# Maxout over three products: one product moved behind the maximum, its share of the output through a matrix formed on chip, and a new order of the whole program

## The chip, the core and the metric

The kernel runs on one core of a Trainium2 chip. The metric is the time of one execution on the device, in microseconds (us). TensorE (PE) multiplies matrices into PSUM, VectorE (DVE) and ScalarE (ACT) work on PSUM and SBUF, GpSimd (POOL) works on SBUF and issues those transfers that change the type, SyncE (SP) issues transfers and transposing transfers.

## The reference

There are 8 batches (B), 8 heads (H), 512 rows of x and 32 rows of state per batch and head, 64 columns. All inputs and the output are float32; the kernel computes in bfloat16 and accumulates in float32.

```python
a  = softmax(x @ state.T / 8)           # per batch and head: 512 x 32
xread = a @ state                        # 512 x 64
a2 = softmax(state @ x.T / 8)           # 32 x 512
sread = a2 @ x                           # 32 x 64
t  = concat([xread, sread], rows)        # heads side by side: 8*544 rows of 512
h  = maximum(maximum(t @ w1, t @ w2), t @ w3)     # 768 columns
out = h @ w_out                          # 4352 rows of 512 columns
```

## The kernel before

The eight batches' xread rows (512 per batch) and the 256 state rows of all batches take two paths.

**Rows of x.** The kernel never forms xread. For a batch it multiplies the states with the weights, G = state @ [w1 w2 w3] for each head (`g_slice`, `g_run`, line 363: eight small matmuls of 64 x 32 tiles side by side), copies G from PSUM to bf16 (lines 381, 403, 406), and then layer 1 is G times the turned softmax weights aT. The 768 columns are six *slices* of 128. For a slice `layer1` makes three products of 512 columns, each of two matmuls (line 416), into three PSUM banks. `max_first` copies the first to SBUF on ACT (line 431); `max_second` takes the maximum with the second on DVE (line 436); `max_third` with the third (line 440), into `ht`. `layer2` (line 447) then makes an output tile of 128 rows as six matmuls over the slices, one PSUM bank; `layer2_out` copies it to SBUF (line 454), and stores take it out.

**Before that**, per batch: x is loaded with a cast by POOL (lines 163, 168), turned by a transposing DMA on SP (line 249; batches 0 and 1 on PE, line 237), multiplied with the states to scores (line 262), exponentiated on ACT (line 269); sums and reciprocals on DVE (276, 278); weights `a` on POOL (line 284), turned into aT by another transposing DMA (line 302). `sread` (line 327) makes the state rows, with a copy of x padded by ones on POOL (line 311); they are scaled, turned by DMA and placed in `atp`.

**State rows.** All 256 go together through layer 1 (`layer1_states`, four matmuls of 256 columns for each of three products and six slices) and layer 2 at the end.

**The order** of every engine's work is written out by hand as a text: FIRST for the start, EACH once per batch 2 to 6, LAST for the end. Each word is one of the functions in `table`. An engine executes its instructions in the order of that text, and waits where an operand or a buffer is not ready; so do the transfers of a queue behind each other. `busy n` is n filler matmuls on zeros (line 211). PSUM has four single banks and two pairs; BANKS and PAIRS name the one that each use takes. The weights come by POOL's queue in column slices (`lw`, line 179), `w_out` by one transfer behind them (`lwo`, line 184), x of batches 2 and up between them.

At the end a matmul with ones gathers a flag that decides about a second path for extreme inputs, which isn't taken here.

Of the kernel before, what the change touches and what calls it, by code (L numbers as in the profile page):

```python
# [17 lines left out]
FIRST = """  # L18
    lst 0 A; lxu 0 0 S; zero; clr 0; clr 1; clr 2; clr 3; warm; lxg 0 1; busy 1; xones 1; ident; busy 1;
    lxg 1 0; busy 1; busy 1; stc 0 D; busy 1; busy 1; busy 1; busy 1; busy 1; lxg 1 1; stt 0; busy 2;  # L20
    cxu 0 0 D; xt 0 0; stp 0 A; busy 1; xt 0 1; busy 1; xtc 0 0 D; lw 0 2 1; lw 0 2 2; xtc 0 1 D;
    busy 1; sc 0 0; busy 1; lw 0 1 0; busy 1; sc 0 1; lw 1 3 0; ex 0 0; busy 1; busy 1; xt 1 0; sum 0 0;
    lw 2 3 1; busy 1; ex 0 1; sum 0 1; xt 1 1; busy 1; xtc 1 0 AD; busy 1; lw 2 3 2; busy 1; xtc 1 1 A;
    busy 1; wt 0 0 P; wt 0 1 P; xones 0; sc 1 0; ex 1 0; busy 1; sc 1 1; at 0 0; atc 0 0 A; sr 0;
    busy 1; sum 1 0; lw 3 4 0; at 0 1; lst 1 A; lw 3 6 2; lw 3 6 1; ex 1 1; wt 1 0 D; g 0 0; gc 0 0 D;
    busy 1; sum 1 1; g 1 0; sr 1; atc 0 1 A; lw 4 6 0; wt 1 1 P; at 1 0; srs 0; g 1 1; g 0 1; stc 1 P;
    l1 0 0; gc 1 1 D; gc 1 0 A; g 1 2; g 0 2; atc 1 0 A; busy 1; gc 0 1 A; m0 0 0; at 1 1; lxg 2 1;
    srs 1; ma 0 0; l1 0 1; lxg 2 0; gc 0 2 A; l1 0 2; atc 1 1 D; l1 1 0; m0 0 1; m0 0 2; lwo; m0 1 0;
    gc 1 2 A; mb 0 0; xtd 2; l1 1 1; g 0 3; m0 1 1; lst 3 S; lst 2 A; ma 0 1; gc 0 3 A; g 1 3; pad 2;
    stt 1; gc 1 3 A; mb 0 1; ma 0 2; mb 0 2; ma 1 0; mb 1 0; l1 1 2; ma 1 1; g 0 5; m0 1 2; ones; g 0 4;  # L30
    mb 1 1; stp 1 DA; l1 0 3; gc 0 4 A; ma 1 2; g 1 4; gr 2 1792 2304; gc 0 5 D; m0 0 3; mb 1 2; l1 1 3;
    l1 0 5; gc 1 4 A; gr 2 0 512; g 1 5; m0 1 3; ma 0 3; mb 0 3; ma 1 3; l1 1 4; grc 2 1792 2304 A;
    mb 1 3; m0 0 5; gr 2 1280 1792; stc 2 P; lxg 3 1; gr 2 512 1024; ma 0 5; l1 0 4; stt 2; sc 2 -;
    gc 1 5 A; m0 1 4; grc 2 0 512 D; mb 0 5; lxg 3 0; ma 1 4; grc 2 1280 1792 AD; m0 0 4; ma 0 4;
    mb 0 4; mb 1 4; xtd 3; l2 0 3; l2 0 1; ex 2 -; l1 1 5; stp 2 A; l2c 0 3 D; stc 3 P; l2 0 2; sum 2 -;
    l2c 0 1 D; stt 3; l2 0 0; m0 1 5; ma 1 5; l2c 0 2 A; grc 2 512 1024 D; wt 2 - P; sr 2; mb 1 5;
    srs 2; gr 2 1024 1280; l2c 0 0 D; so 0 0 2 P; lx 4; so 0 2 4 P; stp 3 A; grc 2 1024 1280 A; atd 2;
"""
EACH = """
    pad 1; gr 1 1792 2304; gr 1 0 512; grc 1 1792 2304 AD; l2 -1 0; l2 -1 1; l1 0 0; grc 1 0 512 D;  # L40
    l2c -1 0 A; m0 0 0; sc 1 -; l2 -1 3; gr 1 1024 1280; ex 1 -; xtd 2; gr 1 1280 1792; l2c -1 1 D;
    ma 0 0; gr 1 512 1024; mb 0 0; sr 1; grc 1 1024 1280 A; l1 0 1; l1 0 2; sum 1 -; l1 0 3; srs 1;
    l1 0 5; l2c -1 3 A; m0 0 1; m0 0 2; ma 0 1; mb 0 1; ma 0 2; m0 0 3; mb 0 2; srt -2; ma 0 3;
    wt 1 - P; m0 0 5; mb 0 3; l2 -1 2; grc 1 1280 1792 A; grc 1 512 1024 A; ma 0 5; mb 0 5; l2c -1 2 D;
    l1 0 4; so -1 2 4 P; m0 0 4; ma 0 4; lx 3; mb 0 4; atd 1; ap -2 A; so -1 0 2 P;
"""
LAST = """
    srt 6; l1 7 0; srt 7; l2 6 0; l1 7 2; m0 7 0; l1 7 3; l1 7 4; ap 7 D; m0 7 2; srt 5; ap 6 A; ma 7 0;
    m0 7 3; mb 7 0; ap 5 A; l2c 6 0 D; ma 7 2; l2 6 1; l1s 0; l2 6 2; m0 7 4; mb 7 2; l1 7 1; l2c 6 1 A;
    ma 7 3; m0 s 0; l2c 6 2 A; l1s 2; l1 7 5; ma 7 4; mb 7 4; look; ma s 0; m0 7 1; m0 s 2; mb s 0;  # L50
    so 6 2 3 S; m0 7 5; mb 7 3; l1s 1; ma 7 1; mb 7 1; ma s 2; mb s 2; ma 7 5; m0 s 1; ma s 1; l1s 5;
    so 6 0 1 S; mb 7 5; l2p 7 2 384 512; l1s 3; m0 s 5; ma s 5; mb s 1; m0 s 3; mb s 5;
    l2pc 7 2 384 512 A; l2p 7 0 384 512; l2p 7 3 256 512; sop 7 2 384 512 P; ma s 3; l2p 7 2 128 384;
    mb s 3; l2p 7 0 0 128; l2pc 7 0 0 128 A; l2pc 7 3 256 512 D; l2p 7 1 0 128; l2p 7 3 0 256;
    l2pc 7 0 384 512 D; flag; l2pc 7 1 0 128 A; l2pc 7 2 128 384 A; l1s 4; m0 s 4; l2 6 3;
    sop 7 0 0 128 P; ma s 4; sop 7 0 384 512 P; mb s 4; l2p s 0 256 512; so 6 1 2 P; l2 s 1;
    sop 7 3 256 512 A; l2c 6 3 D; l2p 7 2 0 128; sop 7 1 0 128 S; l2p s 0 0 256; so 6 3 4 A;
    l2pc 7 3 0 256 D; l2pc s 0 256 512 D; sop s 0 256 512 A; l2pc 7 2 0 128 A; l2p 7 1 128 384;
    sop 7 2 0 128 A; l2p 7 0 256 384; l2p 7 1 384 512; l2pc s 0 0 256 A; l2p 7 0 128 256;
    l2pc 7 1 128 384 A; l2c s 1 D; sop 7 3 0 256 S; sop 7 2 128 384 P; l2pc 7 0 256 384 D;  # L60
    sop 7 1 128 384 A; l2pc 7 1 384 512 D; sop 7 1 384 512 A; l2pc 7 0 128 256 D; sop 7 0 128 256 A;
    sos 1 S; sop s 0 0 256 S; sop 7 0 256 384 S; hold; vl;
# [6 lines left out]
"""  # L69
PAIRS = """  # L70
    0101100101 1010010010 1010101010 1010101010 10
# [4 lines left out]
def kernel(  # L76
# [35 lines left out]
    times = {"D": nc.vector.tensor_mul, "P": nc.gpsimd.tensor_mul}  # L112
    queue = {"S": nc.sync, "P": nc.gpsimd, "A": nc.scalar}
# [9 lines left out]
    w_sb = data.tile([128, HS, 3, d_ff], BF16, name="w")  # L123
# [10 lines left out]
    xT, e, a, aT, G, ht, osb, xp = {}, {}, {}, {}, {}, {}, {}, {}  # L134
    open_ps = {}

    def new(d, b, shape, name, bufs=2):
        d[b] = work.tile(shape, BF16, tag=name, bufs=bufs, name=name)


    homes = {n: iter("".join(t.split())) for n, t in (("b", BANKS), ("w", PAIRS))}
# [28 lines left out]
    def load_x_uncast(b, g, q):  # L170
        o = work.tile([128, J, d_model], F32, tag="osb", bufs=3, name="osb")
        x_f[b, g] = o.rearrange("p j f -> p (j f)")[:, 0:HS * J * D].rearrange("p (s jd) -> p s jd", s=HS)
        queue[q].dma_start(out=x_f[b, g], in_=x_heads(b, g))
# [4 lines left out]
    def load_w(m0, m1, i):  # L178
        nc.gpsimd.dma_start(  # L179
            out=w_sb[:, :, i, m0 * 128:m1 * 128],  # L180
            in_=(moe_w1, moe_w2, moe_w3)[i].rearrange("(kk p) f -> p kk f", p=128)[:, :, m0 * 128:m1 * 128])

    def load_wout():
        nc.gpsimd.dma_start(out=wout_sb, in_=moe_w_out.rearrange("(kk p) f -> p kk f", p=128))
# [46 lines left out]
    def x_turn(b, g):  # L231
        if g == 0:
            new(xT, b, [128, H, 2, 128], "xT", bufs=3)
# [7 lines left out]
    def x_turned(b, g, c):  # L241
        p, w = open_ps.pop(("x", b, g)), HS // len(c)
# [4 lines left out]
    def x_turn_dma(b):  # L247
        new(xT, b, [128, H, 2, 128], "xT", bufs=3)
        nc.sync.dma_start_transpose(out=xT[b].rearrange("p h j t -> p (h j) t"), in_=x_sb[b][:, 0:XW])

# [3 lines left out]
    def scores(b, g=None):  # L254
        if not g:
            new(e, b, [128, J, 2, HS, Ns], "e")
# [11 lines left out]
    def exps(b, g=None):  # L268
        nc.scalar.activation(out=parity(e[b], g), in_=open_ps.pop(("s", b, g)), func=AF.Exp, scale=scale)  # L269
# [10 lines left out]
    def weights(b, g, c):  # L280
        if not g:
            new(a, b, [128, J, 2, HS, Ns], "a")
# [7 lines left out]
    def a_turn(b, g):  # L290
        if g == 0:
            new(aT, b, [128, J, 2, 128], "aT", bufs=3)
# [4 lines left out]
    def a_turned(b, g, c):  # L297
        copier[c](out=aT[b][:, :, g, :], in_=open_ps.pop(("a", b, g)))

    def a_turn_dma(b):  # L300
        new(aT, b, [128, J, 2, 128], "aT", bufs=3)
# [4 lines left out]
    def pad(b):  # L306
        xp[b] = work.tile([128, HS, J, 2 * D + 2], BF16, tag="xp", name="xp")
# [7 lines left out]
    def sread(b):  # L315
        w = D + 1 if b in xp else 2 * D
        p = open_ps["r", b] = bank([128, 2, w], F32, "psr")
        for j in range(J):
            for g in range(2):
                for s in range(HS):  # L320
                    if b in xp:
                        both = xp[b][:, s, j, g * D:g * D + D + 1]
                    else:
# [4 lines left out]
                        p[32 * s:32 * s + 32, g], e[b][:, j, g, s, :], both,  # L328
# [31 lines left out]
    def g_mm(b, p, f):  # L360
        for s in range(HS):
            for g in range(2):
                nc.tensor.matmul(  # L363
                    p(s, g), bd(b, 2 * s + g)[64 * g:64 * g + 64, g, :], f(w_sb[64 * g:64 * g + 64, s]),
                    start=True, stop=True, tile_position=(64 * g, 32 * s))

    def new_g(b):
        if b not in G:
            new(G, b, [128, 2, 3, d_ff], "G", bufs=3)


# [26 lines left out]
    def g_ran(b, c0, c1, c):  # L398
# [5 lines left out]
        else:  # L404
            for g in range(2):
                copier[c[g % len(c)]](out=v[:, g], in_=ps[g][:, 0:c1 - c0])
# [271 lines left out]
```

## Time and profile before

| | |
|---|---|
| time, median of 3 runs (lowest to highest) | 152.66 us (152.51 to 152.88) |
| span of the profiled execution, first to last instruction | 151.4 us |
| PE busy | 146.4 us (97%) |
| DVE busy | 118.9 us (79%) |
| ACT busy | 82.8 us (55%) |
| POOL busy | 57.0 us (38%) |
| moved by DMA | 22.29 MB |

Times in a view of the profile are microseconds from the span's start, unless marked as ns. The profiled execution is one of the program's; its own time isn't recorded beside its span, so that the median, 1.24 us above the span, stands for it. Matmuls are pipelined: the mean duration of one, 379 ns, is longer than the distance from one to the next, which the chain of waits shows. The lines themselves stand in the prediction.

### The profile page before, as it was taken

The page shows a single profiled execution, that of the slowest core. Times are in us where ns is not written, and L with a number is a line of the kernel's source. Part 1 is how long each engine was busy: PE and PEld are TensorE (multiplying, and loading weights), DVE is VectorE, ACT ScalarE, POOL GpSimd, SP SyncE. Part 2 cuts the span into 40 slices and gives each one's busy share as a digit, 9 for nine tenths or more (in the row PEclk, how much of TensorE's full clock was granted, in tenths as well). Part 3 has the DMA queues.
Part 4 walks back from the last instruction along what each step waited for, and adds up shares of the span by engine and source line. Part 5 has one row for each costly group of instructions (what it writes and reads, how often), then busy time and mean ns, then how long its engine had stood idle before and what let it go on. Part 6 is the DMA issues. An engine that isn't in the chain of part 4 may idle for free.

```text
span 151.4 us, 3635 instructions
## 1 busy us (share of the span) xinstructions
PE 146.4 (97%) x1431; PEld 73.8 (49%) x1431; DVE 118.9 (79%) x204; ACT 82.8 (55%) x143; POOL 57.0 (38%) x79
## 2 busy tenths in 40 slices
PE   6999799999999999999999999999999999999992
PEld 2566343335445443544354435443544446679771
DVE  6477698999977898879987988798879887675353
ACT  3368558976364665466646664666466653331220
POOL 6979650561528505540554046414331200001500
PEclk9999999999999999999999999999999999999999
DMA  3999999979737979999589749974503250300455
GB/s 115 211 189 195 207 198 195 151 149 139 139 74 167 230 59 265 129 223 132 155 124 230 144 130 140 232 122 141 218 0 78 68 226 4 122 18 17 175 180 196
DMA packets 39108, 22.29 MB, mean 147 GB/s; under 512 B 23072, under 2 KB 36896, under 8 KB 39088
## 3 DMA queue, kind: packets, MB, share of 16 engines
q0 software_dynamic: 15872, 13.96, 48.7%
q1 hardware_dynamic: 21776, 6.82, 23.4%
q10 hardware_dynamic: 1440, 1.25, 2.7%
q8 instruction: 12, 0.20, 0.5%
q14 instruction: 8, 0.07, 0.2%
HBM read 15.20 MB, written 8.91 MB: 159 GB/s over the span
## 4 chain that ended last, share of the span: by engine, by line
PE 86%; DMA 6%; POOL 4%; issue 1%; DVE 1%; POOLq 0%
PE pw L416 46%; PE po L447 25%; DMA w<-in_moe_w_dram 6%; PE pg L363 5%; PE po L462 4%; POOL w L179 2%; PE ps L262 2%; PE psr L327 2%; POOL x L168 1%; PE pgh L363 1%; PE pt L222 1%; DVE held L522 0%; PE idle L520 0%; PE idle L211 0%; DVE osb L466 0%
## 5 line engine op out<-in xcount | busy, mean ns | idle before, releaser
L416 PE MATMUL pw<-aT,G 128*128 128x512 bf16 x288 | 66.8, 379 | 0.0
L431 ACT CAST t<-pw 128x512 bf16<-128x512 f32 (+1 forms) x54 | 30.4, 564 | 28.9 <-PE pw L416 27.2
L416 PEld LDWEIGHTS <-G 128*128 128x128 bf16 x288 | 27.2, 98 | 33.2 <-issue 1.9
L436 DVE TENSOR_TENSOR t<-t,pw 128x512 bf16<-128x512 bf16 (+1 forms) x54 | 35.4, 655 | 9.5 <-ACT t L431 7.4
L447 PE MATMUL po<-wout,ht 128*128 128x512 bf16 x168 | 39.9, 379 | 0.0
L440 DVE TENSOR_TENSOR ht<-t,pw 128x512 bf16<-128x512 bf16 x48 | 32.9, 687 | 4.3
L447 PEld LDWEIGHTS <-ht 128*128 128x128 bf16 x168 | 15.3, 98 | 19.0 <-issue 1.7
L284 POOL TENSOR_TENSOR a<-e,rden 128x1024 bf16<-128x1024 bf16 (+1 forms) x9 | 14.5, 1620 | 24.1 <-ACT osb L454 11.1
L477 POOL DMA_DIRECT2D out_dram<-osb x13 | 7.4, 572 | 30.5 <-ACT t L431 27.5
L403 ACT CAST G<-pg 128x1024 bf16<-128x1024 f32 (+1 forms) x17 | 14.3, 875 | 1.3 <-PE pg L363 1.3
L311 POOL COPY xp<-x 128x1024 bf16<-128x1024 bf16 x12 | 12.3, 1062 | 5.5 <-DMA x<-in_x_dram 5.5
L454 DVE COPY osb<-po 128x512 f32<-128x512 f32 x16 | 10.9, 684 | 2.4 <-PE po L447 2.3
L276 DVE TENSOR_REDUCE seen<-e 128x32 f32<-128x1024 bf16 (+1 forms) x10 | 10.0, 999 | 3.6 <-ACT e L269 3.6
L403 DVE CAST G<-pg 128x1024 bf16<-128x1024 f32 (+1 forms) x13 | 12.2, 972 | 0.7 <-ACT G L403 0.7
L454 ACT COPY osb<-po 128x512 f32<-128x512 f32 x13 | 7.7, 593 | 8.9 <-PE po L447 8.9
L269 ACT ACTIVATE e<-ps 128x1024 bf16<-128x1024 f32 (+1 forms) x10 | 8.5, 854 | 6.6 <-PE ps L262 6.4
L363 PE MATMUL pg<-w,bd 64*32 64x512 bf16 (+1 forms) x288 | 10.8, 362 | 0.9 <-DMA w<-in_moe_w_dram 0.9
L211 PE MATMUL idle<-zero 128*128 128x512 bf16 x27 | 10.0, 477 | 1.3 <-DVE zero L187 1.3
L472 POOL DMA_DIRECT2D out_dram<-osb x4 | 2.2, 544 | 19.4 <-ACT osb L466 19.4
L381 ACT CAST G<-pg 128x768 bf16<-128x768 f32 x9 | 7.1, 801 | 3.3 <-PE pg L363 3.1
L416 PE MATMUL pw<-atp,w 128*128 128x256 bf16 x72 | 8.7, 272 | 0.0
L416 PEld LDWEIGHTS <-w 128*128 128x128 bf16 x72 | 6.9, 98 | 1.5
(70 smaller groups left out, 116.0 us busy)
## 6 DMA issues: line engine op xcount, KB each, us to landing
out_dram<-osb POOLq DMA_DIRECT2D x12, 512.0 KB, 3.5
x<-in_x_dram POOLq DMA_DIRECT2D x4, 512.0 KB, 7.3
x<-in_x_dram POOLq DMA_DIRECT2D x7, 256.0 KB, 5.5
w<-in_moe_w_dram POOLq DMA_DIRECT2D x4, 256.0 KB, 7.5
w<-in_moe_w_dram POOLq DMA_DIRECT2D x2, 384.0 KB, 7.9
wout<-in_moe_w_out_dram POOLq DMA_DIRECT2D x1, 768.0 KB, 11.6
out_dram<-osb SPq DMA_DIRECT2D x3, 256.0 KB, 2.4
osb<-in_x_dram SPq DMA_DIRECT2D x1, 512.0 KB, 4.0
```

Source lines behind the costliest of these rows:

```text
L211: nc.tensor.matmul(p, zero[:, 0:128], zero, start=True, stop=True)
L276: nc.vector.reduce_sum(out=den, in_=parity(e[b], g), axis=AX.X)
L284: times[c](out=parity(a[b], g).rearrange("p j g s n -> p j (g s) n"), in0=parity(e[b], g).rearrange("p j g s n -> p j (g s) n"), in1=rdens ...
L311: nc.gpsimd.tensor_copy(out=xp[b][:, :, :, g * (D + 1):g * (D + 1) + D], in_=v[:, g])
L363: nc.tensor.matmul(p(s, g), bd(b, 2 * s + g)[64 * g:64 * g + 64, g, :], f(w_sb[64 * g:64 * g + 64, s]), start=True, stop=True, tile_positi ...
L403: copier[c[g]](out=v[:, g:h], in_=p[:, g:h, 0:c1 - c0])
L416: nc.tensor.matmul(pw[i][:, 0:n], lhs(i, k), rhs(k), start=(k == 0), stop=(k == nk - 1))
L431: nc.scalar.copy(out=t0s[b, m][:, 0:n], in_=open_ps["l", b, m][0][:, 0:n])
L436: nc.vector.tensor_max(t1s[b, m][:, 0:n], t0s.pop((b, m))[:, 0:n], open_ps["l", b, m][1][:, 0:n])
L440: nc.vector.tensor_max(ht[b][:, m, :], t1s.pop((b, m))[:, 0:n], open_ps.pop(("l", b, m))[2][:, 0:n])
L447: nc.tensor.matmul(p, ht[b][:, m, j * 128:(j + 1) * 128], wout_sb[:, m, :], start=(m == 0), stop=(m == NM - 1))
L454: copier[c[i]](out=o[:, j, i * w:i * w + w], in_=p[:, i * w:i * w + w])
```

## The change

The maximum of three is written as max(p1, p2, p3) = p1 + max(0, p2 - p1, p3 - p1), with p1 = t @ w1. The differences come from differences of weights, W2 - W1 and W3 - W1, and what p1 contributes to the output is t @ (W1 @ Wout).

- `subtract_w` subtracts w1 from w2 and w3 on DVE, in place, in four pieces (columns 0 to 128, 128 to 256, 256 to 512, 512 to 768). The tile `wm` holds both differences and, in its last 512 columns, M1 = W1 @ Wout.
- `w1_turn` turns w1 on PE (six groups of four transposes), `product` makes M1 by 24 matmuls, and copies bring both to SBUF.
- G has 2 x 768 + 512 = 2048 columns in place of 2304: per batch four runs of 512; in batches 0 and 1 the first run comes as two half slices.
- `layer1` makes two products a slice, into two banks. `max_second` is one instruction, the maximum of the second product, zero and the copy of the first; `max_third` is gone.
- `layer2` takes two more matmuls per tile ahead of the six, aT with the M1 part of G (four more for the state rows: atp with M1).
- The scores are stored with their row blocks in another order (`turned`).
- The order is written anew as one text, PLAN, for all batches, with new lists of banks and, new, of the SBUF buffer that each tile takes (PLACES). Layer 2 of a batch, layer 1 of the next and G of the one after are mixed in another way than before, the loads are issued in another order, and 18 filler matmuls stand at the start in place of 27.

```diff
-    w_sb = data.tile([128, HS, 3, d_ff], BF16, name="w")
+    wm = data.tile([128, HS, 2 * d_ff + d_model], BF16, name="wm")
+    wd = wm[:, :, 0:2 * d_ff].rearrange("p s (r i c) -> p s r i c", i=2, c=256)
...
+    def subtract_w(m0, m1, c):
+        w = (m1 - m0) * 128
+        v = wd[:, :, m0 // 2, :, m0 % 2 * 128:m0 % 2 * 128 + w]
+        minus[c](
+            out=v, in0=v, in1=w1()[:, :, m0 * 128:m1 * 128].unsqueeze(2).to_broadcast((128, HS, 2, w)))
+
+    def w1_turn(m):
+        p = open_ps["w1", m] = bank([128, HS, 128], BF16, "pt")
+        for kk in range(HS):
+            nc.tensor.transpose(p[:, kk, :], w1()[:, kk, m * 128:m * 128 + 128], ident)
...
+    def product(kk):
+        p = open_ps["m1", kk] = bank([128, d_model], F32, "pm")
+        for m in range(NM):
+            nc.tensor.matmul(p, w1(True)[:, m, kk * 128:kk * 128 + 128], wout_sb[:, m, :],
+                             start=(m == 0), stop=(m == NM - 1))
...
+    def maxout(b, m, n, lhs, rhs, nk):
+        pw = open_ps["l", b, m] = [bank([128, 512], F32, f"pw{i}") for i in range(2)]
+        for i in range(2):
+            for k in range(nk):
+                nc.tensor.matmul(pw[i][:, 0:n], lhs(i, k), rhs(k), start=(k == 0), stop=(k == nk - 1))
...
-        nc.vector.tensor_max(t1s[b, m][:, 0:n], t0s.pop((b, m))[:, 0:n], open_ps["l", b, m][1][:, 0:n])
-
-    def max_third(b, m):
-        nc.vector.tensor_max(ht[b][:, m, :], t1s.pop((b, m))[:, 0:n], open_ps.pop(("l", b, m))[2][:, 0:n])
+        nc.vector.scalar_tensor_tensor(
+            out=ht[b][:, m, :], in0=open_ps.pop(("l", b, m))[1][:, 0:n], scalar=0.0,
+            in1=ts.pop((b, m))[:, 0:n], op0=ALU.max, op1=ALU.max)
...
+            steps = [(aT[b][:, turned(j), k, :], G[b][:, k, f]) for k in range(2)]
+        steps += [(ht[b][:, m, t], wout_sb[:, m, c0:c1]) for m in range(NM)]
```

The start of the new order, as far as the prediction speaks of it (`lw a b i`: columns of w1, w2 or w3; `df`: subtraction; `gs`, `gr`: matmuls of G; `l1`, `l2`: the layers; `m1`: product; `xtd`: turning x by DMA; `sc`: scores):

```
lw 0 1 2; lw 0 1 0; lw 0 1 1; ... lw 1 2 2; lw 1 2 0; lw 1 2 1; ... lw 2 4 2; ... df 0 1 D; ... lw 2 4 0;
... gs 0 0; at 0 1; gs 1 0; ... lw 2 4 1; ... lw 4 6 0; ... l1 0 0; ... lwo 0 6; df 1 2 D; ... gr 2 0; gs 0 1;
... sr 1; at 1 0; at 1 1; gs 1 1; w1t 3; ... l1 0 1; ... w1t 2; ... df 2 4 D; ... l1 1 1; ... gr 0 1; ... gr 1 1;
w1t 5; l1 1 0; ... l1 0 2; ... gr 2 1; l1 0 3; ... lw 4 6 2; lw 4 6 1; ... w1t 4; l1 1 2; ... lx 2; ... xtd 2;
m1 3; m1 1; m1 2; ... df 4 6 D; ... gr 0 2; gr 1 2; m1 0; ... l1 0 4; l1 0 5; ... gr 0 3; gr 1 3; ... l1 1 3;
... l2 0 0; l1 1 4; sc 2 -; ... lx 3; ... l2 0 3; l1 1 5; xtd 3; sc 3 -; lx 7; lx 4; ...
```

More of the change, by code (lines that the diff above doesn't have):

```diff
@@ L132, with w1, buffer, new @@
     flag = data.tile([128, 1], I32, name="flag")
-    xT, e, a, aT, G, ht, osb, xp = {}, {}, {}, {}, {}, {}, {}, {}
+    w1s = {}
+    def w1(turned=False):
+        if turned not in w1s:
+            shape = [128, NM, d_model] if turned else [128, HS, d_ff]
+            n = "w1T" if turned else "w1"
+            w1s[turned] = buffer(shape, BF16, "osb", n, n)
+        return w1s[turned]
+    xT, eT, e, a, aT, G, ht, osb, xp = {}, {}, {}, {}, {}, {}, {}, {}, {}
     open_ps = {}
-    def new(d, b, shape, name, bufs=2):
-        d[b] = work.tile(shape, BF16, tag=name, bufs=bufs, name=name)
     homes = {n: iter("".join(t.split())) for n, t in (("b", BANKS), ("w", PAIRS))}
+    places = {}
+    for line in PLACES.split(";"):
+        name, *each = line.split()
+        places[name] = dict(p.split(":") for p in each)
+    def buffer(shape, dtype, tag, key, name=None):
+        n = places[tag][str(key)] if places else str((B if key == "s" else key) % 2)
+        return work.tile(shape, dtype, tag=tag + n, bufs=1, name=name or tag)
+    def new(d, b, shape, name):
+        if b not in d:
+            d[b] = buffer(shape, BF16, name, b)
     def bank(shape, dtype, name):
@@ L247, in x_turn_dma, with turned @@
     def x_turn_dma(b):
[L248 removed]
+        new(xT, b, [128, H, 2, 128], "xT")
         nc.sync.dma_start_transpose(out=xT[b].rearrange("p h j t -> p (h j) t"), in_=x_sb[b][:, 0:XW])
+    def turned(j):
+        return j % 2 * 2 + j // 2
     def parity(v, g):
@@ L306, in pad @@
     def pad(b):
-        xp[b] = work.tile([128, HS, J, 2 * D + 2], BF16, tag="xp", name="xp")
+        new(xp, b, [128, HS, J, 2 * D + 2], "xp")
         nc.gpsimd.memset(xp[b][:, :, :, D:D + 1], 1.0)
@@ L410, in maxout @@
-    def maxout(b, m, n, lhs, rhs, nk, by_k=False):
-        if m == 0 and b not in ht:
-            new(ht, b, [128, NM, n], "ht" if b != "s" else "hts", bufs=4 if b != "s" else 1)
-        pw = open_ps["l", b, m] = [bank([128, 512], F32, f"pw{i}") for i in range(3)]
-        for i, k in [(i, k) for k in range(nk) for i in range(3)] if by_k else [
-                (i, k) for i in range(3) for k in range(nk)]:
-            nc.tensor.matmul(pw[i][:, 0:n], lhs(i, k), rhs(k), start=(k == 0), stop=(k == nk - 1))
@@ L442, in layer2, with new_out @@
     def layer2(b, j):
+        p = open_ps["o", b, j] = bank([128, d_model], F32, "po")
+        layer2_mm(b, j, p, 0, d_model)
+    def new_out(b):
         if b not in osb:
-            osb[b] = work.tile([128, J, d_model], F32, tag="osb", bufs=3, name="osb")
-        p = open_ps["o", b, j] = bank([128, d_model], F32, "po")
-        for m in range(NM):
-            nc.tensor.matmul(p, ht[b][:, m, j * 128:(j + 1) * 128], wout_sb[:, m, :],
-                             start=(m == 0), stop=(m == NM - 1))
+            osb[b] = buffer([128, J, d_model], F32, "osb", b)
```

324 lines of the change are left out of this document (181 added, 143 removed), and 3 rows, old and new, of the table BANKS.

## The prediction, on record before the run

> **What bounds the kernel now.** I read the page from the top: the busy shares, the slices, then the chain of waits, and last the groups. The first fence is the page's own.
>
> ```profile
> span 151.4 us, 3635 instructions
> ...
> PE 146.4 (97%) x1431; PEld 73.8 (49%) x1431; DVE 118.9 (79%) x204; ACT 82.8 (55%) x143; POOL 57.0 (38%) x79
> ...
> PE   6999799999999999999999999999999999999992
> ...
> PEclk9999999999999999999999999999999999999999
> DMA  3999999979737979999589749974503250300455
> ```
>
> PE is full in all slices but the first, one at 17 us and the last; the DMA engines are full from the second slice to the eighth, up to 30 us. So a shorter list of PE work shortens the kernel only from where PE stops waiting for loads. The chain of waits, in order of time, shows where that is (start, length, what; x counts instructions).
>
> ```profile
> 8.17 9.70 DMA w<-in_moe_w_dram
> ...
> 17.91 0.52 PE pg L363 x16
> ...
> 18.97 5.20 PE pw L416 x24
> ...
> 28.20 0.50 PE pg L363 x16
> ...
> 35.98 2.59 PE po L447 x12
> ...
> 41.16 0.22 PE pt L222 x4
> ...
> 42.68 0.38 PE psr L327 x30
> 43.30 0.43 PE pg L363 x16
> ...
> 47.72 0.47 PE ps L262 x16
> ...
> 55.83 1.29 PE po L447 x6
> ...
> 58.42 0.56 PE pg L363 x16
> ...
> 64.73 0.23 PE pgh L363 x8
> ...
> 71.08 1.29 PE po L447 x6
> ...
> 136.68 1.31 PE pw L416 x12
> ...
> 148.20 0.02 issue
> ```
>
> Up to 17.9 us the chain hangs on weights; from there to 148.2 us it is PE without a gap; then come 3.2 us of last copies and stores. These rows also give the prices. A 512-column matmul: 2.59/12 = 0.216 us. A 256-column one of the state rows: 1.31/12 = 0.109. A transpose: 0.22/4 = 0.055. A group of eight G matmuls: 0.43 to 0.56 for two groups, so 0.25, and 0.23 for one with only 256 columns; the group costs about the same whatever its width. Scores of a batch 0.47, its sread 0.38. As a test of the prices, one batch of the steady part runs from 55.83 to 71.08, 15.25 us; it holds 60 wide matmuls (12.96), five G groups (0.23+0.43+0.56 = 1.22), 0.47 and 0.38, together 15.03. The real pace is 1.015 times the prices.
>
> **What the change does to PE's list.**
>
> - Layer 1 makes two products a slice: 96 of 288 wide matmuls go, 96 x 0.216 = -20.7. State rows: 24 of 72 go, 24 x 0.109 = -2.6.
> - G has 2048 columns in place of 2304. Groups fall from 42 (12 slices and 6 x 5 runs) to 34 (4 half slices, 30 runs): 8 x 0.24 = -1.9.
> - Layer 2 takes two more matmuls per output tile: 8 x 4 x 2 x 0.216 = +13.8; the states 2 x 4 x 0.216 = +1.7.
> - The product of w1 and w_out: 24 x 0.216 = +5.2, and 24 transposes of w1, +1.3.
>
> Sum -3.2 us. Priced in the same way the whole new list, without its 18 filler matmuls, is 131.8 us.
>
> The other engines, by their groups:
>
> ```profile
> L440 DVE TENSOR_TENSOR ht<-t,pw 128x512 bf16<-128x512 bf16 x48 | 32.9, 687 | 4.3
> ...
> L431 ACT CAST t<-pw 128x512 bf16<-128x512 f32 x48 | 28.2, 587 | 24.8 <-PE pw L416 23.8 <-DVE t L436 0.7
> ...
> L276 DVE TENSOR_REDUCE seen<-e 128x32 f32<-128x1024 bf16 x6 | 7.3, 1218 | 1.7 <-ACT e L269 1.7
> ...
> L284 DVE TENSOR_TENSOR a<-e,rden 128x512 bf16<-128x512 bf16 x1 | 0.7, 693 | 0.0
> ```
>
> DVE loses one of two maxima per slice (some 33 us) and gains four subtractions. The remaining maximum is a new operation, with the maximum against zero in it. It has the operands of L440; I take 0.69 us, with 0.69 (one pass) and 1.37 (two) as ends. PE now spends 4 x 0.216 = 0.86 us on a slice; the copy on ACT (0.59) and 0.69 on DVE fit beneath that, and the two banks of a slice return in time. So this step costs nothing while PE covers it; the other end is a rival.
>
> **Where the new order waits.** Nothing of layer 1 can start on a slice before all three weights have landed and DVE has subtracted. Subtracting 1024 elements lies between 0.7 and 1.3 us, 2048 between 1.3 and 2.3: the high ends go by the one comparable DVE row, L284 (0.69 for 512, one element a step, and 1.22 for 1024 in L276), the low ends are half a step an element. I take the high ends, since L284 is the nearest.
>
> The Trainium skill, "VectorE: DVE Perf Modes", section on the perf-mode tier table, gives a tensor_tensor of bf16 from SBUF two elements a cycle, 1224 ns for 2048. By it the larger subtraction would be 1.1 us shorter. No run here shows a subtraction of this kind; the trace's L284 has an f32 operand.
>
> Loads are priced from these rows (first the stretches of time, with DMA share and GB/s at the end; then transfers with KB and us to landing; then POOL and SP).
>
> ```profile
> 8.00:16.00 8.00, 7.98 (x171) 5.21 (x168) 5.97 (x15) 6.63 (x11) 6.26 (x10) 1.00 1.55 196
> 16.00:24.00 8.00, 7.14 (x50) 3.02 (x48) 6.49 (x13) 4.86 (x8) 3.98 (x6) 1.00 1.39 199
> ```
>
> ```profile
> w<-in_moe_w_dram POOLq DMA_DIRECT2D x4, 256.0 KB, 7.5
> ...
> wout<-in_moe_w_out_dram POOLq DMA_DIRECT2D x1, 768.0 KB, 11.6
> ...
> xT<-x SPq DMA_TRANSPOSE x6, 4.8
> ...
> xT<-x SPq DMA_TRANSPOSE x1, 8.3
> ```
>
> ```profile
> 15.58 1.47 PE L416 MATMUL pw<-aT,G 128*128 128x512 bf16 x6
> ...
> 26.35 2.05 POOL L311 COPY xp<-x 128x1024 bf16<-128x1024 bf16 x2 [5.51 <-DMA x<-in_x_dram]
> ```
>
> At 196 GB/s 256 KB take 1.34 us. Before, batch 2's x landed at 26.35 us (POOL waited for it until then), with 3584 KB issued by POOL: 768 of x0 and x1, 2304 of weights, 512 of x2. In the new order POOL's queue has x0 and x1, slices 0 and 1, columns 2 to 4 (2304 KB in all, so landed at 26.35 - 5 x 1.34 = 19.65 us), w1's 4 to 6 and w_out (3328 KB, 25.0), the rest of w2 and w3 (3840 KB, 27.7), x2 (4352 KB, 30.4) and x3 (33.1; with x2's turning passing through the same engines 34.4).
>
> Then the walk:
>
> 1. The first layer-1 slice started at 15.58 us. Now 384 KB of weights come ahead of it where 640 did (-1.34), and the subtraction adds 1.3: 15.6.
> 2. From there to the first run of G that needs columns 2 to 4 there is 4.6 us of work: 20.3. Landed and subtracted they are at 19.65 + 2.3 = 21.9. PE waits 1.6 us.
> 3. To the run for columns 4 to 6 there is 8.5 us x 1.015, so 30.6; the data are there at 27.7 + 2.3 = 30.0, and w_out (25.0) is before its products (26.6). No wait. Of the 131.8 us, 18.0 are done.
> 4. The scores of batch 2 come 7.6 us on, at 38.2. x2 has to be turned by a DMA: 4.8 us in the median, 8.3 for the one that ran beside loads. x3, x7 and x4 are queued behind x2, so I take 8.3: 38.7, a wait of 0.5. The scores of batch 3 would start at 41.8; x3 turned is there at 34.4 + 4.8 to 8.3, so 39.2 to 42.7: no wait to 0.9. I take none.
> 5. From 30.6: 0.5 + (131.8 - 18.0) x 1.015 = 116.0; PE ends at 146.6 us.
> 6. The end has the same kind of steps (a narrow tile of layer 2, a copy, a small store), 3.2 us: span 149.8. With more of batch 6's stores late, 2.8 to 4.2 are the ends.
>
> Span to time was 152.66 - 151.42 = 1.24 us, so **151.0 us**, against the median 152.66 of three runs (152.51 to 152.88). PE's list gives 3.2 us; half of that is paid back by the waits at 20 and 38 us. The filler matmuls (27 before, 18 now) stand where PE waits anyway and have no price; their cover gone, each is 0.216.
>
> **Rivals.**
>
> - *The loads are no wait at all*: subtractions at their low end (-1.0 at step 2) and the turned x in 4.8 us (-0.5): 149.5. For it: the median of the six turnings is 4.8, and only one of them is known to have met such a load. Chance 0.22.
> - *x3's turning takes the place of the removed work, and it is slower.* SP issues one turning after the other, and the loaded one held SP for 4.75 us:
>
> ```profile
> 26.38 4.75 SPq L249 DMA_TRANSPOSE xT<-x  x1
> ```
>
>   If x3's load shares with x2's turning, it lands at some 35.6; turned in 8.3 us it is there at 43.9 instead of 41.8, and the time is 151.0 + 2.1 = 153.1. It decides from 1.7 us of further wait. For it: the DMA engines have more queued at that point than before. Against: the DMA row of the page falls to 7 and 3 tenths between 38 and 45 us, so the queue runs out at about that time. Chance 0.20.
> - *PE's clock falls.* The first nine fillers ran at 4.02/9 = 0.447 us, later ones at 0.216:
>
> ```profile
> 1.27 4.02 PE L211 MATMUL idle<-zero 128*128 128x512 bf16 x9 [1.27 <-DVE zero L187]
> ```
>
>   If a wait at 20 or 38 us grew to 3.4 us (2.9 more than the 0.5) and as long a stretch then ran at half pace (1.7 lost), it would be 151.0 + 4.6 = 155.6. Against: the page's granted clock is full in every slice. That such a window of idling halves the clock is what the Trainium skill, "TensorE: Matmul & The Clock Gate", Part 1, states; the trace has no idle stretch of that length and shows only the slow start. Chance 0.03.
> - *Layer 1 does not get shorter*, since the new maximum takes two passes, 1.37 us against PE's 0.86. It would bite where slices stand together (six in a row near the end, with a G copy on DVE): 6 x 0.5, less what the banks buffer, about 2.4: 153.4. Chance 0.05.
>
> The forecast has 0.50, over 150.2 to 152.3.
>
> **How the numbers follow.** Changes within 0.2% (152.35 to 152.97) are about what a measurement of this kernel cannot tell from none. Faster: 0.46 of the forecast's 0.50 and all 0.22, so 0.68. Same: 0.04 and 0.02 of the second rival, 0.06. Slower: 0.18 + 0.03 + 0.05 = 0.26. The range takes in the forecast, the low ends down to 149.0 and the late x3 up to 153.8; the clock, the far side of the slow rivals and a still shorter start, together under 0.2, are left out.
>
> **What would show it.** Layer 1 in the chain at 0.86 us a slice and layer 2 at 1.73 a tile; the new maximum at 0.69; the subtractions at 1.3 and 2.3, or half; PE idle about 1.6 us near 20 and 0.5 near 38, put down to DVE's subtraction and to the turned x; layer 1 starting at 15.6; PE full from 39 us on. A gap of PE after 45 us, a new wait for G's copies in the middle, or a tail over 4.2 us would show me wrong.

## The result, and the profile after

The changed kernel takes 166.87 us (median of four runs, 165.5 to 167.48); beside it the kernel before took 152.71 (152.51 to 152.88). The ratio is 1.090, with an interval of 1.085 to 1.096: 9% slower, where the prediction had 151.0 us and a range up to 153.8.

The page of the changed kernel, the rows that answer to those shown of before. Its profiled execution took 167.48 us.

```profile
span 165.6 us, 3328 instructions
...
PE 147.0 (89%) x1344; PEld 73.4 (44%) x1344; DVE 96.0 (58%) x159; ACT 80.0 (48%) x134; POOL 55.0 (33%) x75
...
PE   5598879798708999999999999999999999999980
...
DMA  4995999999999375972609973603330203001464
```

PE was full from the second slice on but for one slice at 17 us; now its row has a 5 in the second slice, an 8 or a 7 in many more up to the eleventh, and a zero in the twelfth, 45.5 to 49.7 us. DVE lost 23 us of work. The chain of waits (start, length, what; x counts instructions) tells what stands in that hole.

```profile
1.26 4.36 DMA stf<-in_state_dram
...
14.95 2.32 DVE wm L230
...
22.74 12.28 DMA x<-in_x_dram
35.02 0.02 issue
35.04 15.03 DMA xT<-x
50.06 0.05 issue
50.11 1.03 PE ps L326 x16
51.14 3.41 PE po L527 x8
54.56 1.27 PE pw L488 x4
55.83 0.47 PE ps L326 x16
...
78.76 1.73 PE po L527 x8
```

x of batch 2 (`in_x_dram`, issued at 22.74 us, landed at 35.04) is turned by a DMA that takes 15.03 us, and only then can PE make the scores of batch 2, at 50.11. In the kernel before, the slowest of these turnings took 8.3 us and no wait stood behind it. The rows behind it are slow: eight matmuls of layer 2 (L527) take 3.41 us there and 1.73 at 78.76, the scores 1.03 and 0.47, four matmuls of layer 1 (L488) 1.27 and, elsewhere, 0.86. Together that is 2.65 us.

The stretches of time show the same hole from the side of the DMA engines (us, busy time and instructions of PE, PEld, DVE, ACT, POOL, then granted clock, DMA share, GB/s).

```profile
32.00:40.00 8.00, 7.53 (x48) 2.94 (x46) 3.71 (x5) 4.09 (x8) 1.89 (x2) 1.00 1.43 202
40.00:45.00 5.00, 4.37 (x33) 1.61 (x32) 2.95 (x5) 2.09 (x4) 0.98 (x2) 1.00 1.34 167
45.00:50.00 5.00, 0.00 (x0) 0.00 (x0) 0.32 (x1) 0.00 (x0) 0.00 (x0) 0.84 1.74 87
50.00:60.00 10.00, 9.89 (x92) 4.83 (x92) 5.53 (x7) 4.12 (x5) 5.00 (x5) 0.74 0.81 143
```

The clock is down behind the hole (0.74 in the mean of 50 to 60 us). And the DMA engines are at their busiest (1.74) where they move least (87 GB/s): not too little was asked of them, their packets took longer. What was in them is in the rows of SP and POOL in the timeline (start, length, operation).

```profile
35.04 15.04 SPq L312 DMA_TRANSPOSE xT<-x  x2
```

```profile
22.74 3.54 POOL L196 DMA_DIRECT2D x<-in_x_dram  x4
...
40.10 0.88 POOL L196 DMA_DIRECT2D x<-in_x_dram  x1
```

Loads of x2, x3, x7 and x4 (2048 KB) are issued in one go, x6 at 40.10, and the turnings of x2 and x3 pass through the same DMA engines while these loads are in flight.

**Where the time went**, by the walk's own stations, for the profiled execution: scores of batch 2 at 50.1 instead of 38.7 (+11.4); from there to PE's end at 160.7 it is 110.6 instead of 107.9 (+2.7); PE's end to the end of the span 4.9 instead of 3.2 (+1.7); span to time 1.9 instead of 1.24 (+0.6). Sum 16.4; 151.0 + 16.4 = 167.4. The first term has two halves: PE came to the scores of batch 2 at 44.4 where the walk had 38.2 (+6.2), and then waited 5.7 where it had 0.5 (+5.2).

### The profile page after: what moved, and what is told of

The parts are those of the page before. It is cut to its first block, busy times and chain, and to the rows that moved or that the text cites. A ratio compares the mean times of both kernels' runs of the same rounds, so it can differ in the third digit from the quotient of the medians.

```text
span 165.6 us, 3328 instructions
## 1 busy us (share of the span) xinstructions
PE 147.0 (89%) x1344; PEld 73.4 (44%) x1344; DVE 96.0 (58%) x159; ACT 80.0 (48%) x134; POOL 55.0 (33%) x75
## 4 chain that ended last, share of the span: by engine, by line
PE 71%; DMA 19%; DVE 3%; POOL 2%; ACT 1%; issue 0%; ACTq 0%; POOLq 0%
PE po L527 36%; PE pw L488 23%; DMA xT<-x 9%; DMA x<-in_x_dram 7%; PE pg L448 4%; DMA stf<-in_state_dram 3%; PE ps L326 2%; PE idle L275 2%; PE psr L412 2%; DVE wm L230 1%; PE pxt L299 1%; PE pt L286 1%; POOL wm L218 1%; POOL a L370 1%; DVE seen L363 1%; POOL wout L224 1%
## 5 line engine op out<-in xcount | busy, mean ns | idle before, releaser
L527 PE MATMUL po<-wout,ht 128*128 128x512 bf16 (+2 forms) x222 | 48.8, 357 | 0.0
L488 PE MATMUL pw<-aT,G 128*128 128x512 bf16 x192 | 47.7, 382 | 0.8 <-DVE wm L248 0.5
L513 DVE SCALAR_TENSOR_TENSOR ht<-pw,t 128x512 bf16<-128x512 f32 x48 | 31.9, 683 | 14.1 <-ACT t L505 13.9
L527 PEld LDWEIGHTS <-ht 128*128 128x128 bf16 x222 | 21.6, 99 | 21.5 <-issue 2.0
L488 PEld LDWEIGHTS <-G 128*128 128x128 bf16 x192 | 17.9, 99 | 23.6 <-issue 5.3
L527 PE MATMUL po<-G,aT 128*128 128x512 bf16 (+2 forms) x74 | 20.5, 358 | 0.0
L334 ACT ACTIVATE e<-ps 128x1024 bf16<-128x1024 f32 (+1 forms) x10 | 8.5, 853 | 11.1 <-PE ps L326 11.1
L448 PE MATMUL pg<-wm,bd 64*32 64x512 bf16 (+1 forms) x272 | 10.6, 369 | 1.2 <-DVE wm L230 1.1
L326 PE MATMUL ps<-bd,xT 128*128 128x64 bf16 x128 | 5.8, 200 | 5.7 <-DMA xT<-x 5.7
L527 PEld LDWEIGHTS <-aT 128*128 128x128 bf16 x74 | 6.7, 99 | 5.9 <-issue 0.8
L218 POOL DMA_DIRECT2D wm<-in_moe_w_dram x8 | 6.5, 821 | 0.0
```

Of the source, the lines that this page charges most:

```text
L326: nc.tensor.matmul(p[:, 2 * jj:2 * jj + 2, k - gs[0], s, :], xT[b][:, 2 * s + k, jj, :], bd(b, 2 * s + k).rearrange("p c n -> p (c n)"), s ...
L448: nc.tensor.matmul(p(s, g), bd(b, 2 * s + g)[64 * g:64 * g + 64, g, :], f(wm[64 * g:64 * g + 64, s]), start=True, stop=True, tile_position ...
L488: nc.tensor.matmul(pw[i][:, 0:n], lhs(i, k), rhs(k), start=(k == 0), stop=(k == nk - 1))
L513: nc.vector.scalar_tensor_tensor(out=ht[b][:, m, :], in0=open_ps.pop(("l", b, m))[1][:, 0:n], scalar=0.0, in1=ts.pop((b, m))[:, 0:n], op0= ...
L527: nc.tensor.matmul(p, lhs, rhs, start=(i == 0), stop=(i == len(steps) - 1))
```

## The experiments

The names of the theories: **Q**, the turning of x is slow because loads of x are queued beside it; **R**, it is slow in this order by itself; **C**, the clock falls behind the wait and costs more; **S** and **P**, a late state load and gaps in POOL's issues make the start late; **F**, the late flag makes the longer end. Lines in a diff are words of the order; `lx b` is the load of batch b, `pad b` the padded copy, which waits until x of b has landed.

**1. The loads of x4 to x7 later.**

```diff
-lx 3; ... lx 7; lx 4; pad 3; ... lx 6; wt 2 - P; pad 4; ... wt 3 - P; pad 2; lx 5;
+lx 3; ... pad 3; ... wt 2 - P; lx 4; ... wt 3 - P; lx 7; lx 6; pad 4; pad 2; lx 5;
```

> The changed kernel, with x4, x7 and x6 issued by POOL only after the weights a of batches 2 and 3 (x3 stays right behind x2). Theory Q (the turning of x2 took 15.0 us because loads of x that nobody needed yet shared the DMA engines with it): it shares with x3 alone, so 8 to 9 us; the scores of batch 2 start at 43 to 44 us in place of 50.1, PE idles about 0 to 1 us before them in place of 5.7, the granted clock stays at 1.00 (worth 2.6 us), and the time falls from 166.9 to 157 to 159. Theory R (the turning is slow for a reason of its own in the new program, SP or the place of x2's landing): it stays at 15 us and the time at 166 to 168.

Measured: 165.07 us (164.37 to 166.57), ratio 1.079 (1.070 to 1.088). SP's two turnings, in its timeline, and the wait that was left, in PE's:

```profile
33.66 5.52 SPq L313 DMA_TRANSPOSE xT<-x  x2
...
55.74 6.03 SPq L313 DMA_TRANSPOSE xT<-x  x1
```

```profile
67.23 1.04 PE L327 MATMUL ps<-bd,xT 128*128 128x64 bf16 x16 [5.94 <-DMA xT<-x]
68.08 2.80 PE L489 MATMUL pw<-aT,G 128*128 128x512 bf16 x8
```

The turnings of x2 and x3 now held SP for 5.52 us in place of 15.04, though x3's load was still in flight beside x2's (5.0 us to landing), and the wait at the scores of batch 2 was gone. But x7 and x6 were now issued just ahead of x4's turning (at 52.56) and x5 during it; it landed after 11.4 us: the wait of 5.9 us had moved to the scores of batch 4. The mechanism of Q held; the gain did not come.

**2. The kernel before with nothing changed but two loads.** Its x3 and x4 are issued right behind `w_out` (`lwo; lxg 3 1; lxg 3 0; lx 4;`), so that they meet the turning of x2.

> The kernel before, with nothing of the change, but x3 and x4 (1024 KB) issued by POOL right behind w_out, ahead of their place. Theory Q: the turning of x2 grows from 8.3 us to 13 or more, the scores of batch 2, at 35.5 us before, wait until 40 or later, and the time grows from 152.7 to 156 to 160, the more if the clock falls in the wait. Theory R: the turning stays at about 8 us and the time at 152.7 within 0.5.

Measured: 161.31 us (160.43 to 162.88), ratio 1.052 (1.045 to 1.060); the profiled execution took 162.88. Its chain, below the row of the kernel before that answers to its last:

```profile
35.51 0.47 PE ps L262 x16
```

```profile
26.91 15.55 DMA xT<-x
42.50 1.04 PE ps L262 x16
```

Without anything of the change, the same turning takes 15.55 us, the scores start at 42.50 where they were at 35.5, and the time grows by 8.2 us (153.11 beside it; by 7.3 in the shortest execution), more than the 156 to 160 us expected. This decides against R: the slow turning needs nothing of the change.

**3. Fillers in the hole**: 24 filler matmuls ahead of the scores of batch 2 (`busy 24; sc 2 -;`).

> The changed kernel with 24 filler matmuls (5.2 us) on PE right ahead of the scores of batch 2, inside its wait of 5.7 us. They do no work. Theory C (after the wait PE runs at a lower clock for about 6 us, which costs 2.6 us: eight wide matmuls in 3.41 us where 1.73 is usual, four in 1.27, scores in 1.03): the granted clock stays 1.00 through 45 to 60 us, the rows return to 1.73, 0.86 and 0.47, and the time falls by 2 to 3 us, to about 164.3. Its rival (the slow rows are waits for operands that the view does not name): the rows and the time stay.

Measured: 166.54 us (165.31 to 167.07), ratio 1.089 (1.083 to 1.096). PE's timeline:

```profile
42.66 5.34 PE L277 MATMUL idle<-zero 128*128 128x512 bf16 x24
49.04 0.64 PE L328 MATMUL ps<-bd,xT 128*128 128x64 bf16 x16 [1.04 <-DMA xT<-x]
...
53.44 0.64 PE L328 MATMUL ps<-bd,xT 128*128 128x64 bf16 x16 [1.16 <-DMA xT<-x]
```

In the profiled execution (165.31 us, the shortest of the four) the clock stayed at 1.00 through 45 to 60 us and the scores took 0.64 us in place of 1.03, so C is right about the rows. But the scores of batch 3 now waited 1.16 us for x3's turning, which the slow clock had covered before: from the one scores to the other it is 4.40 us in place of 5.72, and not 2.65 less. The median cannot be told from that of the changed kernel, and the 164.3 us expected were missed.

**4. The flag earlier**, its matmul ahead of the last state tile.

> The changed kernel with the matmul that gathers the flag moved ahead of the last state tile of layer 2 (about 4 us before the end of PE's work; it was the last but one). Theory F (the tail of 4.9 us after PE's last tile, where the kernel before had 3.2, and the 1.9 us between span and time are the reading of a flag that is ready only at 161.1 us): span after PE's end falls to 3.2 to 3.7 us, time by 1 to 1.7. Its rival (the last stores are what ends late): the tail stays 4.9 and the time within 0.5.

Measured: 167.38 us (166.25 to 168.24), ratio 1.094. No gain, and from PE's last tile to the end of the span it is 5.9 us where it was 4.9; F fell.

**5 to 8. Loads spread over the batches**, each x one batch ahead of its turning; alone, with the state's first load ahead of ACT's warming, with the weights of columns 2 to 4 ahead of the first weights `a` in POOL's queue, and with both.

```diff
-lx 3; ... lx 7; lx 4; pad 3; ... lx 6; wt 2 - P; pad 4; ... wt 3 - P; pad 2; lx 5; ... pad 5; ... pad 6;
+lx 3; ... pad 3; ... wt 2 - P; lx 4; ... wt 3 - P; pad 2; pad 4; lx 5; ... pad 5; lx 6; ... pad 6; lx 7;
```

> The changed kernel, with the loads of x4 to x7 spread out on POOL's queue: x4 behind the weights a of batch 2, x5 behind the padded copy of x4, x6 behind that of x5, x7 behind that of x6, so that each turning of x has the DMA engines nearly to itself; x3 stays right behind x2. In the kernel with x4, x7 and x6 moved only a little, the wait moved from x2's turning to x4's (11.4 us, PE idle 5.9 us before the scores of batch 4, then slow rows). Theory Q: neither wait remains, no turning but x2's and x3's takes over 6 us, the granted clock is 1.00 in every stretch, and the time falls from 165.1 by 5.9 + 1.6 to about 157.5. Theory R (each turning of the new order is slow at some point by itself): a wait of about 6 us appears again and the time stays over 163.

> As the kernel with the loads of x4 to x7 spread out, and the first state load issued by ACT ahead of the table load, as in the kernel before. In the changed kernel the state landed at 5.6 us in place of 3.6, PE waited 2.5 us for it, and the first slice of layer 1 started at 18.6 in place of 15.6. Theory S (the late state shifts the whole start): the state is there at 3.6 to 4.5, the first slice starts 1 to 2 us earlier, and the time is 1 to 2 us below the spread kernel's. Its rival (the weights, or POOL's weights a, set the first slice): the first slice and the time stay within 0.5.

> As the kernel with the loads of x4 to x7 spread out, and the weight loads of columns 2 to 6 ahead of the products a on POOL that they stood behind. In the changed kernel POOL waited there until 13.8 us for the sums of batch 0, and the DMA engines moved only 55 to 110 GB/s from 11 to 19 us. Theory P (this gap makes all later loads late): DMA runs at 180 GB/s or more through 11 to 19 us, x2 lands at 31 us in place of 34 to 35, the scores of batch 2 start 2 to 3 us earlier, and the time is 2 to 3 us below the spread kernel's. Its rival (PE's own work and DVE set the scores): x2 lands earlier, the scores and the time stay within 0.7.

> The spread kernel with both: the first state load ahead of ACT's table load, and the weight loads ahead of the products a. If S and P add up: 4 us below the spread kernel's time, so about 153, level with the kernel before; if one covers the other, the better of the two, about 155. Faster than the kernel before only if the tail also shortens, which nothing here does.

Measured: 171.89 us (ratio 1.126, 1.120 to 1.132), 170.40 (1.115), 172.52 (1.128) and 169.33 (1.105). The spread kernel was to take 157.5 and was slower than the change itself. Its chain shows why:

```profile
43.09 0.47 PE ps L327 x16
...
57.42 11.13 DMA aT<-a
...
83.42 12.94 DMA xT<-x
```

The scores of batch 2 came at 43.09 without a wait, but POOL now issued x5 at 57.54, just when the weights of batch 3 were being turned (57.42), and x7 at 82.80, just ahead of x6's turning: PE waited 4.0 and 6.5 us, each with a slow stretch behind it. It was so in all four kernels (10.7 to 11.1 us for these weights, 2.7 when nothing is beside them; 12.1 to 13.2 for x6). I had taken it that a single load would cost a few us at most.

The load was not alone there: POOL issued a store of 512 KB right behind x5, and two behind x7. In the changed kernel, with two such stores beside it and no load, x6's turning took 6.4 us, so the load about doubles it. By itself a load costs less: the weights of batch 2 were turned at 48.41, with x4's load issued at 48.33 and nothing else beside them.

```profile
48.33 0.94 POOL L197 DMA_DIRECT2D x<-in_x_dram  x1
```

```profile
48.41 1.23 SPq L388 DMA_TRANSPOSE aT<-a  x1
```

They landed after 7.3 us in place of 2.7, and PE did not wait for them.

The earlier state load moved the scores of batch 2 from 43.09 to 41.83 and was worth 1.5 us, as S said. The order of the weights by itself did nothing: x2's turning began at 30.58 us in place of 34.17, yet the scores stayed at 43.06, so there it was PE's own path that set them, with its waits for DVE. With both, the scores came at 41.08; the two did not give the 4 us hoped for but 2.6.

**9 and 10. The four loads in one piece.** They stand together behind `pad 3`, which waits until x3 has landed, and ahead of the turnings of x4 to x7; the second kernel has the two changes to the start as well.

```diff
-lx 3; ... lx 7; lx 4; pad 3; ... lx 6; wt 2 - P; ... pad 2; lx 5;
+lx 3; ... pad 3; lx 4; lx 5; lx 6; lx 7; wt 2 - P; ... pad 2;
```

> The changed kernel with the loads of x of batches 4, 5, 6 and 7 issued by POOL in one piece right behind the padding of batch 3, which waits until x of batch 3 has landed. The four loads (2048 KB) then stand between about 39 and 50 us, after the turnings of x2 and x3 and before every later turning. Theory Q (a turning is slow when a load of x is queued beside it): scores of batch 2 at 43.1 us, as where only x2 and x3 were loaded early, no wait of PE over 1 us on a turned x or turned weights, granted clock 1.00; the work from there to PE's end is 107.96 us, with a tail of 4.9 and 1.9 between span and time 157.9 us (157 to 160; the upper end if the last of the loads still meets the turned weights of batch 2). Theory R (a turning in this order is slow by itself): still one of 11 us or more, a wait of 4 us or more, and over 165 us.

> As the kernel with all loads behind the padding of batch 3, and with the state's first load ahead of ACT's warming, and the weights of columns 256 to 768 and w_out ahead of the first weights a in POOL's queue. Where the loads were spread, these two together moved the scores of batch 2 from 43.1 to 41.1 us. Theories S and P (a late start and POOL's gap in the loads are what is left of the loss): 155.9 us (154.5 to 158), 2 us under the kernel beside it, and still 3 us over the kernel before. If they are hidden behind the weights anyway: the same as the kernel beside it within 0.5 us.

Measured: 160.98 us (160.38 to 161.03), ratio 1.052 (1.049 to 1.056), and 157.12 us (156.29 to 158.4), 1.030 (1.025 to 1.034). The page of the second, and one row of PE's timeline of the first:

```profile
PEclk9999999999999999999999999999999999999998
DMA  4999999999999993072498636015300302000563
```

```profile
58.62 1.89 PE L490 MATMUL pw<-aT,G 128*128 128x512 bf16 x8 [1.01 <-DMA aT<-a]
```

Moving four loads, and nothing else, gave back 5.9 of the 14.2 us, though the 157 to 160 us expected were missed by one. The loads still met turnings in the first kernel: those of x2 and x3, which ran when they were issued (6.5 and 6.9 us), of the weights of batch 2 (10.2) and of x4 (12.0); PE waited 1.0 us for the weights and 0.7 for x4. In the second, where everything is earlier, no turning of x took over 6.9 us, none of weights over 5.2, and PE waited for none. There the scores of batch 2 start at 40.93 and PE ends at 149.6, 108.7 later: forecast 107.9.

**11. POOL away from the first subtraction**: the two weights `a` of batch 0 on DVE (`wt 0 0 D; wt 0 1 D`).

> The changed kernel with the two weights a of batch 0 multiplied on DVE and not on POOL. If the first subtraction took 2.32 us because POOL worked on SBUF beside it: it takes 0.63 us as the second one, and the first product of layer 1 starts 0.5 to 1 us earlier, at 17.6 to 18.1 us in place of 18.57. If it is slow for another cause (its operands, just landed): still over 2 us. The time as a whole hangs on the turnings, so 165.5 to 167.5 either way.

Measured: 165.09 us, one execution. DVE's timeline of the changed kernel, then of this one:

```profile
14.95 2.32 DVE L230 TENSOR_TENSOR wm<-wm,w 128x1024 bf16<-128x1024 bf16 x1
...
18.90 0.63 DVE L230 TENSOR_TENSOR wm<-wm,w 128x1024 bf16<-128x1024 bf16 x1
...
24.27 1.23 DVE L230 TENSOR_TENSOR wm<-wm,w 128x2048 bf16<-128x2048 bf16 x1
```

```profile
15.27 0.68 DVE L231 TENSOR_TENSOR wm<-wm,w 128x1024 bf16<-128x1024 bf16 x1
```

The subtraction fell to 0.68 us and the first slice of layer 1 moved from 18.57 to 17.27. Not all of that is the subtraction's: PE waited 1.8 us for the state in this execution and 2.5 in the other, and with the same start as the changed kernel the first kernel of experiment 9 has its first slice at 17.93. So the first subtraction had been held up by POOL, not by its operands, and it cost the start some 0.7 us.

**12. Less to store**: the store of the first half of batch 6 is left out, so that part of the output is missing.

> The changed kernel without the store of the first half of batch 6's output (512 KB), so that half a batch of the output is left out. If the end waits for the amount of stores issued in the last 3 us (1216 KB, at the 300 to 350 GB/s of that stretch): from PE's end to the span's end 3.4 us in place of 4.9, and the time 1.5 us shorter, 165.4. If it is the landing of the last small store whatever is beside it: still 4.7 to 5 us.

Measured: 167.87 us, one execution. From 159 to 161 us the DMA engines stood still, and yet PE's end to the span's end was 4.7 us. In this execution the end does not wait for the amount of stores.

**13 and 14. What is left.** The kernel of experiment 10 with the weights `a` of experiment 11, alone and with one narrow store moved ahead of the two stores of state rows (`sop 7 0 0 256 S; sos 1 S; sos 0 S`).

> As the kernel with all loads behind the padding of batch 3 and the earlier start (157.12 us), and with the two weights a of batch 0 multiplied on DVE. In that kernel the scores of batch 2 started at 40.93 us, 2.2 later than the walk of the prediction had them. If the first subtraction's 2.32 us is a part of that delay: it takes 0.65 us, the scores of batch 2 start 0.8 to 1.3 us earlier, at 39.6 to 40.1, and the time is 156.0 us (155.4 to 156.6). If the start hangs on the loads by then and not on DVE: 40.9 and 157.1 as before. By none of them does it reach the kernel before.

> As the kernel beside it, with one of the last narrow stores issued on SP ahead of the two stores of state rows, behind which it waited for the second state tile. If the end hangs on the last issue of SP: that comes 0.55 us earlier, PE's end to the span's end is 4.3 us in place of 4.8, and the time 0.5 us under the kernel beside it. If the end hangs on something else: 4.8 us and no difference beyond 0.2 us.

Measured: 156.3 us (156.06 to 156.9), ratio 1.024 (1.021 to 1.027), and 156.25 us (156.12 to 156.68), 1.023 (1.020 to 1.026). The first time lies in the range expected, but by luck: the scores of batch 2 were to come at 39.6 to 40.1 and stayed at 41.05 (41.03 in the second). In the kernel that they start from, the first subtraction already took only 0.84 us; it lies there beside 0.2 us of POOL's product and 0.6 of its issuing. And with SP's last issue over at 149.83 instead of 150.35 us, the span stayed at 154.2: the end hangs on something else. None of the kernels beats the one before.

## Why the prediction was wrong, step by step

- **Step 4 failed**: "The scores of batch 2 ... x3, x7 and x4 are queued behind x2, so I take 8.3: 38.7, a wait of 0.5". The turning took 15.0 us, the wait was 5.7, and the scores came at 50.1. I had taken the worst of six turnings as the price with loads beside it; in that row the loads beside it were fewer, and the DMA row soon fell to 7 and 3 tenths. Experiment 2 shows that two more loads, in the kernel before, make the same turning 15.55 us, and experiment 1 that it takes 5.0 us in the changed kernel where x3's load alone is beside it. Of the 11.4 us by which the scores were late, 6.7 are the turning and 4.6 the landing of x2. The argument against the rival of x3's turning, that the queue runs out, used the row of before for an order that issues 2048 KB at once.
- **x2 landed late**, at 35.04 against 30.4, which feeds the same step. The sum took POOL's queue as full at 196 GB/s from the first load. But POOL waited 4.46 us for DVE's reciprocals, with loads queued behind its product, and the loads ran at 128 GB/s from 8 to 16 us and at 134 from 16 to 24. POOL's row in the timeline, then the two stretches:

```profile
13.82 1.05 POOL L370 TENSOR_TENSOR a<-e,rden 128x512 bf16<-128x512 bf16 x1 [4.46 <-DVE rden L365]
```

```profile
8.00:16.00 8.00, 7.58 (x118) 5.81 (x115) 5.38 (x11) 5.19 (x9) 3.52 (x6) 1.00 1.21 128
16.00:24.00 8.00, 5.62 (x102) 2.94 (x102) 7.21 (x13) 5.84 (x12) 7.79 (x10) 1.00 1.09 134
```

  Experiment 7 took these loads ahead of the product: x2's turning began at 30.58 us, as forecast within 0.2. By itself that gained nothing, since PE was not there yet.

- **Steps 1 to 3 failed too: they were 3.0, 3.7 and 5.1 us late** (18.57, 25.55 and 35.72 against 15.6, 21.9 and 30.6). Without the long turning PE would still have come to the scores of batch 2 at 44.4, so the two failures lie side by side, and mending the turning alone could not give back the whole. At step 1 the new order has ACT warm its table ahead of the state's load, which is issued at 1.26 instead of 0.82, two at once, and PE waits 2.5 us for the state; I had not walked ACT's queue at all. Then comes the subtraction, 2.32 us instead of 1.3. With the state's load first and the weights ahead of POOL's products the first slice is at 16.0 (experiment 10), as forecast within 0.4.
- **The subtraction's price** was taken from the wrong end. Undisturbed it is 0.63 and 1.23 us, half of my 1.3 and 2.3. That is the rate of the Trainium skill, "VectorE: DVE Perf Modes", perf-mode tier table (1224 ns for 2048); the trace agrees. The disturbed one, 2.32, lay above both ends. The Trainium skill, "SBUF — State Buffer", section "Who interferes with whom", says that a DVE instruction with two inputs in SBUF contends with a GpSimd instruction that reads there; experiment 11 agrees, with 2.32 against 0.68.
- **The clock rival** was right in kind, and its condition was met (3.4 us of wait; here 5.7): the rows behind the hole lost 2.65 us, of which 1.2 stood where a wait would have been. Its chance of 0.03 was too small because the wait was taken too small.
- **Right**: the new maximum takes one pass, as the row of after says, and DVE stays off the path from the scores of batch 2 on (at the start its first subtraction stands in the chain).

```profile
L513 DVE SCALAR_TENSOR_TENSOR ht<-pw,t 128x512 bf16<-128x512 f32 x48 | 31.9, 683 | 14.1 <-ACT t L505 13.9
```

  Layer 1 at 0.86 us a slice and layer 2 at 1.73 a tile, the list of 131.8 us and the factor 1.015 held: 107.9 forecast from the scores of batch 2 on, 107.96 measured when the slow stretch is taken off. That they agree to 0.1 us is luck, since 1.2 us of that stretch covered a wait; the kernels of experiments 10 and 13, without it, have 108.7 and 108.3. The 3.2 us that PE's list gives are a difference of two priced lists, and no run measures them by themselves; the order loses five times as much.
- **The end** took 4.9 us instead of 3.2. F, the amount of stores and SP's last issue were each tried and fell. In the kernel of experiment 13, 2.2 us pass after the last data, with no engine busy; in the kernel before it is 0.4. What ends them is open.
- **Span to time** was 1.9, not 1.24: in all later runs of the kernel before, the time stood 1.8 to 2.0 above the span (152.42 with 150.6, for one), so that its profiled span of 151.4 was of an execution of some 153.3.

Of the 14.2 us, 5.9 are shown to come from the place of four loads (experiment 9), and 3.9 from the start and the order of the first loads, with the wait that this still removes (experiment 10). The kernel with both mended is 6.1 us over the forecast: 2.2 before the scores of batch 2, 0.8 from there to PE's end, 1.6 at the end, 0.7 between span and time, and 0.8 between its profiled execution (156.36) and its median. The 2.2 us are not settled. In the kernel of experiment 13 PE has six waits of 0.2 to 0.7 us between 15 and 42 us, put down to DVE's maxima, copies and products, 2.3 us together; but the walk had waits of 2.1 us of its own there (1.6 and 0.5), which are gone, so that the six explain little of it. The first slice comes 0.4 us late, and the rest is PE's own pace on this stretch, which no experiment has taken apart.

## What to carry to other kernels

Price a transfer that others wait for by what else is in flight when it is issued, not by its mean or its worst row; a load that nobody waits for yet, issued a few us earlier or later, was worth more here than all the arithmetic that was saved. When an order is written anew, walk every queue from its first instruction, ACT's and POOL's too, and ask for each stall in it which transfers it delays. And when a wait shows behind a turning, put the loads where few turnings are: spreading them evenly was worse here than issuing them in one piece.

## What the runs showed of the hardware

- A transposing DMA of 512 KB that lands after 4.2 us at best took 5.0 to 5.2 beside one load of 512 KB that had been issued 8 to 12 us ahead of it (x2 beside x3, experiments 1 and 5 to 8), 12.1 to 13.2 beside a load issued 0.6 us ahead of it and two stores of 512 KB, and 15.0 and 15.6 beside several loads queued ahead of it (the changed kernel and experiment 2). While this lasted in the changed kernel, the DMA engines showed a share of 1.74 and 87 GB/s. One of 256 KB, 2.7 us at best, took 7.3 to 7.4 beside a load alone and 10.7 to 11.1 beside a load and a store. The Trainium skill, "Advanced Engine Details and Errata", section "X-Bar Transpose (TRN2)", has such transfers as fast as regular ones; no run here sets one against a regular copy of the same size beside the same loads.
- DVE and POOL on SBUF: a subtraction of 0.63 us took 2.32 where POOL multiplied and issued loads beside it, and POOL's product 1.30 in place of 1.05 beside DVE's product. Beside 0.6 us of POOL's issuing and 0.2 of a product it took 0.84, so the product is the likelier cause.
- The granted clock fell to half for some 5 us behind a PE idle for 5.7 us, and not where fillers covered it. In experiment 8 it fell behind an idle of 3.6 us (0.50 from 68 to 70 us); behind the 2.5 us at the start of the changed kernel it did not (1.00 from 4 to 10 us). The Trainium skill, "TensorE: Matmul & The Clock Gate", Part 1, has this from some 3.4 us of idling on; the traces agree.
